# Inverse tables turned on GpSimd and transposed behind the filter's transposing DMAs, with another order of staging buffers

## The chip, the cores and the metric

The kernel runs on one core of a Trainium2 chip. The metric is device time in microseconds (us) of one launch. Three runs of the kernel before took 195.03, 194.29 and 194.93 us, so the median is 194.93 us.

The core's engines are named as in the profile: PE is TensorE (matmuls; PEld are its weight loads), DVE is VectorE, ACT is ScalarE, POOL is GpSimd, SP is SyncE, which here only issues DMAs. Each engine works through its own list in order, and waits for the others by semaphores.

## The reference, cut to what matters

With x = q of 2048 rows and 512 columns, in bf16:

```
xn = layernorm(q)
kv = causal_conv4(k, shift_k) * v                    # 4 taps along the sequence, per column
y  = irfft(rfft(kv, 4096) * rfft(ssm_k, 4096))[:2048]  # a long convolution per column
s  = xn * (y + kv * ssm_D)
h  = gelu_tanh(xn @ w_gate) * (xn @ w_up)            # 512 -> 1792
out = q + s * silu(h @ w_down)                       # 1792 -> 512
```

## The kernel before, in words

**Two halves on one PE.** The gated feed-forward part takes the 2048 rows in four quarters `q` of 512 rows and the 1792 columns in 14 tiles `m`. `unit(q, m)` (L1109) makes the gate and the up product in one PSUM bank each; ACT turns the gate bank into `GE` by gelu (L1137), and DVE multiplies the up bank by `GE` into `HT` (L1140), which frees the up bank and the `GE` slot. `down(q)` (L1143) multiplies `HT` by `Wd`. The long convolution is a two-stage Fourier transform made of matmuls. Stage 1 multiplies by `F1`: `stage1_h` (L929) for the filter, in units `H0` to `H7` and `J0` to `J7` (the two halves of the filter's columns), and `stage1_k` (L956) for `kv`. Each unit is copied from PSUM into a staging buffer and sent to HBM (`ZH`, `ZK`); stage 2 reads it back in another order and multiplies by 32x32 tiles of the table `TF` (`fwd`, L1031). The inverse multiplies by the table `MI` (L1094).

**The tables.** DVE makes `TF` (L717). `m_turn` (L726) makes from it `TFA` and `TFB`, four operations of 128x512 elements each, of which the second negates. A transposing DMA on SP turns `TFA` into `MI[:, 0]` and another one turns `TFB` into `MI[:, 1]` (L1036 to L1040); a third makes `G1` from `F1`. All three signal one semaphore, `d_g1`, and `Trk.dma` (L213) lets a DMA wait until the one before it on its semaphore has landed.

**The filter.** Filter rows come as `Hn` (four tiles, in the bytes of `G`). Two of the four are transposed by PE (`HTr`). The other two are copied by ACT into `HP` (L894) and transposed by two DMAs on SP into `HTD` (L899), one for each half `hf`; the `J` units read `HTD`.

**The taps.** SP loads the four taps to all partitions as `SKR`; POOL copies one tap at a time into `SKB[:, j]`, j = 3, 2, 1, 0 (L986). `kshift(i)` (L988) multiplies and adds on DVE for four row tiles: `KAC = KK * SKB3` (L1005), then for j = 2, 1, 0 `KTM = KK * SKBj` (L1009) and `KAC += KTM` (L1011). `KTM` has the same bytes as `SKR`:

```
skr_at = kac_at + 8192          # SKR, 4096 bytes a partition
KAC = new("KAC", [128, 2, 4, DM], BF16)   # 8192 bytes from kac_at
KTM = new("KTM", [128, 1, 4, DM], BF16)   # the 4096 bytes behind them
```

So `Trk._need` (L137) lets the first write of `KTM` wait for the last read of `SKR`, which is the copy of tap 0.

**The order of the work.** Every step is a numbered task. The string `SEQ` (L27) lists all of them in the order in which they are emitted; each engine's list is that order, cut to the engine's tasks. A planner (`Sched.run`, L345) goes through `SEQ` with estimated times, and picks buffer slots and PSUM banks by them: the slot that came free earliest. Loads are issued by SP too (`load`, L594). The tasks that matter here:

- 146, 147, 148, 149 (POOL): the copies of taps 3, 2, 1, 0; 150 (DVE): `KAC` of `kshift(0)`; 151: its first `KTM`; 152: the add behind it
- 402, 404 (PE, DVE): the up product of unit (0, 6) and its product into `HT`; 410 (PE): the up product of unit (0, 8), which the plan puts into the bank that 404 frees; 415 (ACT): the gelu of unit (0, 9), which takes the `GE` slot that 404 frees
- 81 (ACT): `m_turn`
- 61, 62 (SP): the DMAs into `HTD`; 183, 184 (SP): the transposing DMAs from `TFA` and `TFB` into `MI`; 182: the one into `G1`
- 44, 43, 41, 40, 42, 45 (SP): the loads of V2, KK3, Wd0, V1, Wd1, KK4 behind 62; 166 (DVE): `KAC` of `kshift(2)`, which needs KK3

**Staging buffers.** The `H` units use four buffers in tiles 8 to 15 of `X`. The `J` units have four as well, in the order of the list `ast["J"]` (L485): two in `X` (tiles 12 and 14) and two in `G` (tiles 4 and 6, the bytes of an `Hn` tile that PE has read by then). `J` units are evicted in the order 4, 6, 7, 2, 1, 3, 5, 0.

Of the kernel before, what the change touches and what calls it, by code (L numbers as in the profile page):

```python
# [10 lines left out]
ACTF = mybir.ActivationFunctionType  # L11
# [14 lines left out]
ORDER = "x02 h0 h1 x22 w0 w1 h2 h3 D0 w2 s0 k0 v0 x1 w3 k1 v1 d0 d1 k2 v2 k3 v3 x2 x3"  # L26
SEQ = (  # L27
# [22 lines left out]
)  # L50
NF_BANKS = 4
ISSUE = 470.0
# [29 lines left out]
class Trk:  # L82
# [29 lines left out]
    def res(self, name, ap):  # L112
        t = ap.tensor
        tn = type(t).__name__
        if tn.startswith("SB"):
            key = "SB"
            addr = self.nc.lookup_mloc(t).addr
        else:
            assert tn.startswith("PS")
            key = "PS:" + t.name  # L120
            addr = 0
        esz = mybir.dt.size(ap.dtype)
        pairs = [list(q) for q in ap.ap]
        pst, pn = pairs[0]
        pstart = ap.offset // pst if pst else 0
        inner = ap.offset - pstart * pst
        hi = sum(st * (n - 1) for st, n in pairs[1:])
        r = Res(name, key, pstart, pstart + pn, addr + inner * esz, addr + (inner + hi + 1) * esz)
        lst = self.res_by_key.setdefault(key, [])
        for o in lst:  # L130
            if o.plo < r.phi and r.plo < o.phi and o.blo < r.bhi and r.blo < o.bhi:
                o.ovl.append(r)
                r.ovl.append(o)
        lst.append(r)
        return r
# [263 lines left out]
def build_kernel(nc, A_q, A_k, A_v, A_shift_k, A_ssm_k, A_ssm_D, B_w_gate, B_w_up, B_w_down, out):  # L399
    with ExitStack() as es0:  # L400
# [11 lines left out]
        def new(name, shape, dt):  # L412
            h = at(name, shape, dt, place["at"])
            place["at"] += size(shape, dt)
            return h
# [4 lines left out]
        X = new("X", [128, NT, DM], BF16)  # L420
# [24 lines left out]
        G = new("G", [128, NT, DM], BF16)  # L445
# [36 lines left out]
        def quarter(T, j):  # L482
            return T[:, j:j + 2, :].rearrange("p x (y d) -> p (x y) d", d=256).rearrange("p (r c) d -> p r c d", c=2)

        ast = {"H": [quarter(X, j) for j in (8, 10, 12, 14)], "J": [quarter(T, j) for T, j in ((X, 12), (X, 14), (G, 4), (G, 6))],  # L485
               "K": [AST[:, j, :, :, :] for j in range(2)] + [ASX[:]]}

        ZH = nc.dram_tensor("ZH", [NG, 128, DM], BF16, kind="Internal")
# [15 lines left out]
        trk = Trk(nc, block)  # L504
        S = Sched()
# [18 lines left out]
        R_F1, R_G1, R_MF, R_MFA, R_MFB = res("F1", F1[:]), res("G1", G1[:]), res("TF", TF[:]), res("TFA", TFA[:]), res("TFB", TFB[:])  # L524
# [82 lines left out]
        def copy(e, h, o, i, scale=1.0):  # L607
            if e == "ACT":
                return h.activation(o, i, ACTF.Copy, scale=scale)  # L609
            if scale != 1.0:  # L610
                return h.tensor_scalar(o, i, scale, None, ALU.mult)
            return h.tensor_copy(o, i)  # L612
# [15 lines left out]
        bF1, bG1, bMF, bMI, bid, bSKB = B("F1"), B("G1"), B("TF"), [B(f"MI{i}") for i in range(2)], B("id"), [B(f"SKB{j}") for j in range(4)]  # L628
# [97 lines left out]
        def m_turn(e):  # L726
            tf, ta, tb = (T[:].rearrange("p g (b c) -> p (g b) c", c=2) for T in (TF, TFA, TFB))
            for o, i, f, R in ((ta[:, :, 0], 0, 1.0, R_MFA), (ta[:, :, 1], 0, -1.0, R_MFA), (tb[:, :, 0], 1, 1.0, R_MFB), (tb[:, :, 1], 1, 1.0, R_MFB)):
                trk.op("ACT", lambda h, o=o, i=i, f=f: h.activation(o, tf[:, :, i], ACTF.Copy, scale=f), r=[R_MF], w=[R])

        bFP, bQ, bMQ, bMF2 = B("fp"), B("q"), B("mq"), B("mf2")
        bFM = B("fm")
# [159 lines left out]
        for hf in range(2):  # L892
            for k in range(2):
                h_perm.append(op([("ACT", act(1024, True)), ("DVE", dve(1024, 1))], lambda e, h, hf=hf, k=k: copy(e, h, HP[:, 8 * hf:8 * hf + 8, k, :], Hn[:, 2 + k, :].rearrange("p (a t) -> p t a", t=NT)[:, 8 * hf:8 * hf + 8, :]),  # L894
                                 r=[bHn[2 + k]], w=[bHP[hf]], rr=[R_Hn[2 + k]], ww=[R_HP[hf]]))
        for hf in range(2):
# [8 lines left out]
           r=[bHD, *[bHTr[k][0] for k in range(2)]], w=[bFold], rr=[R_D, *R_HTr[0]], ww=R_HTr[0])  # L905
        op([("DVE", 420.0)], lambda e, h: h.tensor_tensor(HD0, HD0, Drow[:, 256:512], ALU.add),
           r=[bHD, bHTD[0]], w=[bFoldD], rr=[R_D, R_HTD[0]], ww=[R_HTD[0]])
        ln(0)
        S.add([("ACT", 2400.0)], m_turn, r=[bMF], w=[bMF2])
        for t in tm_tasks:  # L910
            S.behind(t, [d for b in bXN[0:4] for d in b.writers])
        xn_transpose(0)
# [310 lines left out]
        for j in range(6):  # L1223
# [7 lines left out]
                  r=[b2], w=[B(f"out{j}")], nbytes=262144)  # L1231
# [12 lines left out]
def bass_recurrent_scan__ssm_conv_h3__glu_gated_geglu__prompt_kernel(  # L1244
    nc: bass.Bass,
    A_q: bass.AP,
    A_k: bass.AP,
    A_v: bass.AP,
    A_shift_k: bass.AP,
    A_ssm_k: bass.AP,  # L1250
    A_ssm_D: bass.AP,
    B_x: bass.AP,
    B_w_gate: bass.AP,
    B_w_up: bass.AP,
    B_w_down: bass.AP,
    out: bass.AP,
):
    build_kernel(nc, A_q, A_k, A_v, A_shift_k, A_ssm_k, A_ssm_D, B_w_gate, B_w_up, B_w_down, out)
# [28 lines left out]
```

## Time and profile before

| what | value |
|---|---|
| median of three runs | 194.93 us (194.29 to 195.03) |
| span of the profiled execution | 193.3 us, so about 1.6 us of a run lie around the span |
| busy: PE, DVE, ACT, POOL | 188.6, 160.0, 125.4, 13.9 us |
| granted TensorE clock | 1.000 |
| HBM read, written | 27.39 MB, 14.68 MB |

The page gives one profiled execution. A row of a timeline has the start in us from the span's start, the length in us, the engine, the line of the kernel, the operation, what it writes and reads, and how many instructions were merged; in brackets stands the idle time of the engine just before it and what ended that. Rows named SPq or ACTq are issues of DMAs. In a row of a tile, three numbers are the shortest, the median and the longest in ns.

### The profile page before, as it was taken

How to read it: one execution, taken by the hardware profiler on the slowest of the kernel's cores; microseconds unless marked ns; L12 is line 12 of the kernel's file. 1: busy time of each engine (PE TensorE's matmuls, PEld its weight loads, DVE VectorE, ACT ScalarE, POOL GpSimd, SP SyncE). 2: the span in 40 equal slices, each digit the busy share in tenths (PEclk: the TensorE clock that was granted, in tenths of full speed). 3: DMA queues.
4: the chain of work that ended last, by engine and by line, in shares of the span. 5: the costliest groups of instructions: out<-in, count | busy, mean ns of one | idle time of the engine just before them, and what ended most of it. 6: DMA issues, size and time to landing. Idle time of an engine off the chain costs nothing.

```text
span 193.3 us, 3502 instructions
## 1 busy us (share of the span) xinstructions
PE 188.6 (98%) x1377; PEld 85.6 (44%) x1377; DVE 160.0 (83%) x245; ACT 125.4 (65%) x170; POOL 13.9 (7%) x32
## 2 busy tenths in 40 slices
PE   7899999999999999999999999999999999999993
PEld 2685544444444444443434433433444334444452
DVE  6699789998999995877888789878897863588993
ACT  6787999969885987868548766856577431232121
POOL 5412420000000000020300000000000000000000
PEclk9999999999999999999999999999999999999999
DMA  5999999999999679999999991984805345939333
GB/s 175 311 307 349 377 400 347 157 249 372 375 374 354 196 264 259 390 323 305 218 285 230 338 320 59 288 276 147 264 10 195 106 140 153 389 112 353 132 139 136
DMA packets 45958, 49.19 MB, mean 254 GB/s; under 512 B 12787, under 2 KB 39671, under 8 KB 45942
## 3 DMA queue, kind: packets, MB, share of 16 engines
q1 hardware_dynamic: 37366, 42.67, 70.1%
q10 hardware_dynamic: 8576, 6.29, 10.3%
q8 instruction: 11, 0.18, 0.4%
q14 instruction: 5, 0.04, 0.1%
HBM read 27.39 MB, written 14.68 MB: 218 GB/s over the span
## 4 chain that ended last, share of the span: by engine, by line
PE 93%; DMA 4%; SPq 1%; DVE 1%; ACT 0%; issue 0%
PE psall L618 86%; PE psall L1028 5%; DMA Hn<-in_A_ssm_k_dram 4%; PE psall L854 1%; SPq L590 1%; PE psall L878 1%; DVE G L1175 0%; DVE G L1174 0%; ACT G L1172 0%
## 5 line engine op out<-in xcount | busy, mean ns | idle before, releaser
L618 PE MATMUL psall<-xnT,Wu 128*128 128x512 bf16 (+1 forms) x232 | 55.8, 372 | 0.0
L618 PE MATMUL psall<-xnT,Wg 128*128 128x512 bf16 (+1 forms) x232 | 55.3, 372 | 0.0
L618 PE MATMUL psall<-Wd,HT 128*128 128x512 bf16 (+2 forms) x238 | 52.0, 367 | 0.0
L1140 DVE TENSOR_TENSOR HT<-psall,GE 128x512 bf16<-128x512 f32 x54 | 36.7, 685 | 15.8 <-PE psall L618 15.4
L1137 ACT ACTIVATE GE<-psall 128x512 bf16<-128x512 f32 x54 | 31.7, 601 | 13.1 <-PE psall L618 12.9
L618 PEld LDWEIGHTS psall<-Wd,HT 128*128 128x128 bf16 x238 | 22.4, 98 | 25.9 <-issue 1.1
L618 PEld LDWEIGHTS psall<-xnT,Wg 128*128 128x128 bf16 x232 | 21.9, 98 | 25.4 <-issue 1.3
L618 PEld LDWEIGHTS psall<-xnT,Wu 128*128 128x128 bf16 x232 | 21.6, 98 | 25.9 <-issue 3.5
L609 ACT ACTIVATE X<-psall 128x1024 bf16<-128x1024 f32 (+1 forms) x18 | 15.1, 843 | 3.3 <-DMA ZH<-X 1.9
L609 ACT ACTIVATE HS<-psall 128x1024 bf16<-128x1024 f32 x14 | 13.7, 1022 | 4.4 <-PE psall L1028 4.4
L1164 ACT ACTIVATE G<-psall 128x512 bf16<-128x512 f32 x12 | 7.0, 598 | 12.9 <-PE psall L618 12.4
L1011 DVE TENSOR_TENSOR KAC<-KAC,KTM 128x2048 bf16<-128x2048 bf16 x12 | 14.6, 1217 | 0.1
L1009 DVE TENSOR_TENSOR KTM<-KK,SKB 128x2048 bf16<-128x2048 bf16 x12 | 14.6, 1217 | 0.0
L609 ACT ACTIVATE BO<-psall 128x1024 bf16<-128x1024 f32 x9 | 9.1, 1022 | 8.2 <-PE psall L1028 7.7
L609 ACT ACTIVATE KB<-psall 128x1024 bf16<-128x1024 f32 x11 | 11.0, 1021 | 3.6 <-PE psall L1028 3.6
L609 ACT ACTIVATE AST<-psall 128x1024 bf16<-128x1024 f32 x12 | 12.4, 1033 | 0.7 <-PE psall L618 0.5
L612 DVE CAST BO<-psall 128x1024 bf16<-128x1024 f32 x7 | 8.5, 1224 | 3.7 <-PE psall L1028 3.7
L821 DVE BATCH_NORM_STATS2 stats<-X 128x6 f32<-128x512 bf16 x16 | 10.3, 675 | 1.1 <-DMA X<-in_A_q_dram 1.1
L1172 ACT ACTIVATE G<-psall 128x512 bf16<-128x512 f32 (+2 forms) x5 | 2.6, 512 | 13.1 <-PE psall L618 13.1
L1091 DVE TENSOR_TENSOR HW<-KB,HW 128x1024 bf16<-128x1024 bf16 x16 | 10.9, 682 | 0.0
L1091 DVE TENSOR_TENSOR HS<-KB,HS 128x1024 bf16<-128x1024 bf16 x16 | 10.8, 682 | 0.0
L1166 DVE SCALAR_TENSOR_TENSOR G<-G,psall 128x512 bf16<-128x512 bf16 x12 | 7.8, 680 | 2.0 <-ACT G L1164 2.0
(83 smaller groups left out, 175.6 us busy)
## 6 DMA issues: line engine op xcount, KB each, us to landing
BH<-ZH SPq DMA_DIRECT2D x8, 512.0 KB, 6.1
HW<-HS SPq DMA_DIRECT2D x16, 256.0 KB, 3.2
BK<-ZK SPq DMA_DIRECT2D x8, 512.0 KB, 5.1
ZI<-BO ACTq DMA_DIRECT2D x16, 256.0 KB, 2.8
BI<-ZI SPq DMA_DIRECT2D x8, 512.0 KB, 4.2
ZK<-AST SPq DMA_DIRECT2D x6, 512.0 KB, 4.1
Hn<-in_A_ssm_k_dram SPq DMA_DIRECT2D x4, 512.0 KB, 8.4
KK<-in_A_k_dram SPq DMA_DIRECT2D x4, 512.0 KB, 8.6
```

What stands on the lines that cost most here:

```text
L609: return h.activation(o, i, ACTF.Copy, scale=scale)
L612: return h.tensor_copy(o, i)
L618: return h.matmul(o, lhsT=l, rhs=r, start=st, stop=sp)
L821: t_stats[t] = op([("DVE", 670.0)], lambda e, h, t=t: h.bn_stats(stats[:, t, :], X[:, t, :]), r=[bX[q][t % 4]], w=[bst[t]], rr=[R_X[t]], w ...
L1009: op([("DVE", dur)], lambda e, h, j=j, m=m: h.tensor_tensor(KTM[:, m.slot, :, :], kk(j), sk(j), ALU.mult), r=need + [bSKB[j], a], w=[m], r ...
L1011: op([("DVE", dur)], lambda e, h, m=m: h.tensor_tensor(KAC[:, a.slot, :, :], KAC[:, a.slot, :, :], KTM[:, m.slot, :, :], ALU.add), r=[m], ...
L1028: trk.op("PE", lambda h: h.matmul(ps(s, i)[b, :], lhsT=wt(col)[a, :], rhs=data(col)[a, :], start=n < 16, stop=n >= len(todo) - 16, tile_po ...
L1091: return hd.tensor_tensor(o, flat(KB, kb[h]), o, ALU.mult)
L1137: op([("ACT", act(512))], lambda e, h: h.activation(GE[:, g.slot, :], bank(pg), ACTF.Gelu_apprx_tanh), r=[pg], w=[g], rr=lambda: R_bank(pg ...
L1140: op([("DVE", dve(512, 1))], lambda e, h: h.tensor_tensor(HT[:, q % 2, m, :], bank(pu), GE[:, g.slot, :], ALU.mult), r=[pu, g], w=[bHT[q][m]],
L1164: op([("ACT", act(n))], lambda e, h, g=g, pc=pc: h.activation(g, pc(), ACTF.Tanh, scale=0.5), r=[p], w=[bt], rr=lambda p=p: R_bank(p), ww= ...
L1166: op([("DVE", dve(512, 1))], lambda e, h, g=g, pc=pc: h.scalar_tensor_tensor(out=g, in0=g, scalar=1.0, in1=pc(), op0=ALU.add, op1=ALU.mult ...
```

## The change

Three edits. `m_turn` is emitted to POOL instead of ACT, by the helper `copy` (L607), which makes a copy for the factor 1.0 and a `tensor_scalar` with a multiplication for -1.0. In `SEQ`, task 81 goes from behind 430 to between 147 and 148; 183 goes to right behind 61, and 184 to right behind 62. All else in `SEQ` keeps its order (the string is only broken into lines at other places). The `J` units' list of buffers begins with the two in `G`.

```
 SEQ = (
...
-    ... 430 81 477 ...      ... 140 183 45 508 ...      ... 137 184 241 ...
+    ... 396 99 147 81 121 466 148 468 150 ... 149 151 ...
+    ... 417 61 183 423 424 106 429 156 97 114 158 93 60 62 184 431 44 ...
...
-        ast = {"H": [quarter(X, j) for j in (8, 10, 12, 14)], "J": [quarter(T, j) for T, j in ((X, 12), (X, 14), (G, 4), (G, 6))],
+        ast = {"H": [quarter(X, j) for j in (8, 10, 12, 14)], "J": [quarter(T, j) for T, j in ((G, 4), (G, 6), (X, 12), (X, 14))],
...
         def m_turn(e):
             tf, ta, tb = (T[:].rearrange("p g (b c) -> p (g b) c", c=2) for T in (TF, TFA, TFB))
             for o, i, f, R in ((ta[:, :, 0], 0, 1.0, R_MFA), (ta[:, :, 1], 0, -1.0, R_MFA), (tb[:, :, 0], 1, 1.0, R_MFB), (tb[:, :, 1], 1, 1.0, R_MFB)):
-                trk.op("ACT", lambda h, o=o, i=i, f=f: h.activation(o, tf[:, :, i], ACTF.Copy, scale=f), r=[R_MF], w=[R])
+                trk.op("POOL", lambda h, o=o, i=i, f=f: copy("POOL", h, o, tf[:, :, i], f), r=[R_MF], w=[R])
...
-        S.add([("ACT", 2400.0)], m_turn, r=[bMF], w=[bMF2])
+        S.add([("POOL", 2600.0)], m_turn, r=[bMF], w=[bMF2])
```

43 rows, old and new, of the table SEQ are left out of this document.

## The prediction

> **What bounds the kernel now.** I read the page first, its busy times and its chain, and then the table of busy times in stretches of 10 us.
>
> ```profile
> PE 188.6 (98%) x1377; PEld 85.6 (44%) x1377; DVE 160.0 (83%) x245; ACT 125.4 (65%) x170; POOL 13.9 (7%) x32
> ...
> PE 93%; DMA 4%; SPq 1%; DVE 1%; ACT 0%; issue 0%
> ```
>
> ```profile
> 20.00:30.00 10.00, 10.00 (x60) 5.03 (x59) 8.07 (x12) 9.37 (x15) 3.41 (x4) 1.00 1.07 392
> 30.00:40.00 10.00, 10.00 (x52) 4.68 (x50) 10.00 (x12) 10.00 (x13) 0.00 (x0) 1.00 0.98 237
> 40.00:50.00 10.00, 10.00 (x48) 4.54 (x47) 9.17 (x11) 8.26 (x13) 0.00 (x0) 1.00 1.06 331
> 50.00:60.00 10.00, 10.00 (x48) 4.57 (x47) 10.00 (x11) 7.65 (x11) 0.00 (x0) 1.00 1.11 361
> ```
>
> In the second fence the columns after the length are PE, PEld, DVE, ACT and POOL, then the granted clock and the DMA share. PE is the chain, and it is busy in all of each stretch in which the change does anything, at a granted clock of 1.00. The change leaves PE's list as it is. So time that is freed on ACT, or in the DMA queue, has no hole on PE to fill; but each moment for which the change holds PE back is lost for good, because nothing later has slack to give it back. The question is therefore not what ACT saves, but whether anything that PE waits for comes later than it may.
>
> **Part 1: the four operations move from ACT to POOL, between the copies of taps 2 and 1.** What ACT gives up:
>
> ```profile
> L729 ACT ACTIVATE TFA<-TF x2: 774/778/783, 42.7 to 43.5; 128x512 bf16<-128x512 bf16 x2
> ```
>
> Four operations of about 0.78 are 3.1 us of ACT from 42.7 on. PE is full there, so this is worth nothing.
>
> What POOL has, and what DVE does next to it:
>
> ```profile
> 17.09 0.24 POOL L831 TENSOR_SCALAR mv<-mv 128x4 f32<-128x4 f32 x1 [6.45 <-DVE mv L822]
> 17.42 1.05 POOL L832 TENSOR_TENSOR mv<-mv,NHALF 128x4 f32<-128x4 f32 x1
> 21.85 3.41 POOL L986 COPY SKB<-SKR 128x512 bf16<-128x512 bf16 x4 [3.39 <-DMA SKR<-in_A_shift_k_dram]
> ```
>
> ```profile
> L986 POOL COPY SKB<-SKR x4: 637/646/1658, 21.9 to 23.6; 128x512 bf16<-128x512 bf16 x4
> ```
>
> ```profile
> 23.32 1.42 DVE L1005 TENSOR_TENSOR KAC<-KK,SKB 128x2048 bf16<-128x2048 bf16 x1
> 24.66 0.68 DVE L1140 TENSOR_TENSOR HT<-psall,GE 128x512 bf16<-128x512 f32 x1
> 25.30 1.22 DVE L1009 TENSOR_TENSOR KTM<-KK,SKB 128x2048 bf16<-128x2048 bf16 x1
> 27.45 0.69 DVE L1140 TENSOR_TENSOR HT<-psall,GE 128x512 bf16<-128x512 f32 x1 [0.94 <-PE psall L618]
> 28.06 1.22 DVE L1011 TENSOR_TENSOR KAC<-KAC,KTM 128x2048 bf16<-128x2048 bf16 x1
> 29.19 0.68 DVE L1140 TENSOR_TENSOR HT<-psall,GE 128x512 bf16<-128x512 f32 x1
> ```
>
> The copies start 0.58 apart and take 0.64. The last one starts at 23.60 and takes 1.66: it ends at 25.26, as if it had begun only at 24.62, when the `KAC` multiplication that started at 23.32 was about done. So POOL's copy stands still while DVE multiplies two SBUF operands.
>
> The Trainium skill has a rule for that ("SBUF — State Buffer", section "Who interferes with whom"): a DVE instruction with two SBUF inputs and a GpSimd instruction that reads SBUF shut each other out for a whole instruction. The two rows agree with it; by it alone the moved operations could also hold DVE's multiplications back.
>
> Now the wait that matters. The `KTM` row at 25.30 is task 151, and it starts 0.04 after the last copy's end at 25.26. That is no accident: `KTM` has the bytes of `SKR`, so its first write waits for the copy of tap 0, the last on POOL's list, although it needs only tap 2. Behind it on DVE stands 404 (27.45), the product that frees the bank of the up product 410. In the kernel before, DVE has 0.94 to spare ahead of 404. The change puts four more operations ahead of the copy of tap 0.
>
> POOL's list worked out anew, with X for the second operation, the `tensor_scalar`:
> - Taps 3 and 2 as before. Operation 1 takes the place of tap 1: 23.02 to 23.66.
> - Operation 2 writes the same tile and waits for operation 1. A POOL operation that waits for the one before starts 0.09 after its end (17.09 + 0.24, then 17.42), so at 23.75; the `KAC` multiplication then holds it to 24.62, as it held tap 0. It ends at 24.62 + X.
> - Operation 3 ends 0.58 later (25.20 + X), operation 4 waits for it and ends at 25.93 + X.
> - Tap 1 ends at 26.51 + X, tap 0 at 27.09 + X. `KTM` starts at 27.13 + X instead of 25.30.
>
> DVE has nothing else that it may do: 404 stands behind `KTM`. DVE's next operation starts 1.13 after such a multiplication (28.06, then 29.19), and 404 takes 0.69, so 404 ends at 28.95 + X.
>
> ```profile
> 29.02 1.03 PE L618 MATMUL psall<-xnT,Wu 128*128 128x512 bf16 x4
> ```
>
> ```profile
> 74.40 1.02 ACT L609 ACTIVATE ASX<-psall 128x1024 bf16<-128x1024 f32 x1 [0.81 <-PE psall L618]
> ```
>
> ```profile
> 75.47 0.28 PEld L618 LDWEIGHTS psall<-V,F 128*128 128x128 bf16 x2 [0.15 <-ACT ASX L609]
> ```
>
> The PE row is 410. How soon PE follows: where a load waited for ACT's end at 75.42, it started at 75.47; with some 0.2 from a load to its matmul, I estimate 0.25 from the freeing to the matmul. PE would start 410 at 29.20 + X, and it started at 29.02. **The stall is 0.18 + X.**
>
> X is not in the trace: no POOL `tensor_scalar` with 512 elements.
>
> ```profile
> L663 POOL TENSOR_SCALAR ident<-K 128x128 bf16<-128x128 int32 x1 | 0.6, 568 | 0.0
> ...
> L831 POOL TENSOR_SCALAR mv<-mv 128x1 f32<-128x1 f32 x4 | 0.9, 224 | 3.4 <-DVE mv L822 3.4
> ```
>
> From 1 to 128 elements the `tensor_scalar` grows by 344 ns, 2.7 ns an element; 512 elements would take 1.6 us. From below, the copy of as many elements takes 0.64. It can't take less than a copy, which leaves no gain here. The first is a comparison of int32 and the second is no arithmetic; a bf16 multiplication lies between them, and I take the middle, X = 1.1. The stall is 0.82 with the low end, 1.28 with mine, 1.8 with the high one. The three copies of `m_turn` step over every second element on both sides, the tap copies over four on one side; I take the tap's 0.64 for them, and if each took 0.2 more, 0.6 would be added, which is the upper part of my range.
>
> The Trainium skill's "GPSIMD Engine Reference", section "Engine selection", calls one-input operations on GpSimd roughly line-rate; by that X would be at the low end, and the time 195.75. No run here shows it for a `tensor_scalar`.
>
> What is late behind it: 415 waits for the `GE` slot that 404 frees, so ACT falls back by about as much, and DVE too. Their products then lie against a PE that is late by the same amount, so I count the stall once. DVE's later multiplications meet POOL no more, as POOL is done.
>
> **Part 2: the transposing DMAs.** They are behind the filter's on SP, ahead of six loads.
>
> ```profile
> 32.08 6.18 SPq L899 DMA_TRANSPOSE HTD<-HP  x2
> 38.30 1.51 SPq L590 DMA_DIRECT2D V<-in_A_v_dram  x1
> 39.87 0.48 SPq L590 DMA_DIRECT2D KK<-in_A_k_dram  x1
> ...
> 44.33 5.69 SPq L1039 DMA_TRANSPOSE MI<-TFA  x1
> ...
> 54.57 2.61 SPq L1039 DMA_TRANSPOSE MI<-TFB  x1
> ...
> 61.81 1.32 SPq L1039 DMA_TRANSPOSE G<-F  x1
> ```
>
> ```profile
> KK<-in_A_k_dram SPq DMA_DIRECT2D x1, 512.0 KB, 6.3
> ```
>
> ```profile
> HTD<-HP SPq DMA_TRANSPOSE x2, 5.3
> ```
>
> ```profile
> 36.00:37.00 1.00, 1.00 (x6) 0.42 (x5) 1.00 (x2) 1.00 (x3) 0.00 (x0) 1.00 0.26 54
> ```
>
> ```profile
> 48.67 1.22 DVE L1005 TENSOR_TENSOR KAC<-KK,SKB 128x2048 bf16<-128x2048 bf16 x1
> 49.81 1.22 DVE L1011 TENSOR_TENSOR KAC<-KAC,KTM 128x2048 bf16<-128x2048 bf16 x1
> 50.94 0.68 DVE L1140 TENSOR_TENSOR HT<-psall,GE 128x512 bf16<-128x512 f32 x1
> ```
>
> ```profile
> 52.77 1.03 PE L618 MATMUL psall<-xnT,Wg 128*128 128x512 bf16 x4
> ```
>
> An issue into `MI` took 2.61 and 5.69 in a loaded queue, the four times smaller one into `G1` 1.32; the queue is lighter here (a DMA share of 0.26 at 36), so I take 1.3 to 2.6. The two issues move the loads back by 2.6 to 5.2. The second one also waits for the first one's landing on their one semaphore, and the loads stand behind that wait: with 5.3 to landing, as for `HTD`, it lies mostly under the issues of the first (1.3 or more) and of the second `HTD` DMA (half of 6.18), and about 1 is left over. So the loads are issued up to 6.2 later.
>
> KK3 has the nearest need: 39.87 + 6.3 is 46.2, and DVE multiplies by it at 48.67, which leaves 2.5. DVE's next product ends at 51.62, its bank is taken at 52.77, and with my 0.25 that leaves 0.9 more until PE feels it. With the forecast's stall, DVE comes 1.3 later by itself. So KK3 may be 4.7 late. Its 6.3 to landing were spent behind the `HTD` transpose and V2; the transposes into `MI` now partly use the idle queue of 36. I expect it to land 2 to 4 later and take zero; the upper bound is 6.2 - 4.7 = 1.5. The other loads are needed later than KK3, and KK4 no longer has the `MI` issue of 5.69 in front of it.
>
> **Part 3: buffers.**
>
> ```profile
> 57.87 1.02 ACT L609 ACTIVATE X<-psall 128x1024 bf16<-128x1024 f32 x1 [0.96 <-DMA ZH<-X]
> ```
>
> ACT waits such as this one, for a staging buffer's store to land, become shorter: J4 and J6, evicted first, take `G` tiles, and their stores find a shorter queue. The reverse, J7 and J2 waiting for an `X` tile, comes later, when more stores have landed. PE is full at 57.87 all the same, and such a wait is under 1 us of an engine that PE doesn't wait for there: zero both ways.
>
> **Sum.** The span of 193.3 becomes 193.3 + 1.3 = 194.6; with the 1.6 us around it that is **196.2 us**, against the median of 194.93 (slower by 0.7%).
>
> **The rivals.** A difference under 0.5% (1.0 us, the runs lie within 0.74) can't be told from none.
>
> *X at its low end.* The stall is 0.82 and the time 195.75, which counts as no change. For it: the copy's row. Against: the 568 ns for 128 elements. 0.18.
>
> *The wait doesn't reach PE*, because the plan's altered times give 410 another bank, or another up product is enough ahead: 194.9. Against it: the bank of 404 is the longest free one in the plan by a step, and an altered POOL time of 0.2 in the plan is small. 0.08.
>
> *KK3 late.* PE's stall comes as in the forecast, and at 50 DVE waits again, for KK3. It decides when the load is issued more than 4.7 later and still takes 6.3; from nothing to 1.5 is added, in the middle 0.8: 197.0. For it: two issues and a landing ahead of it. Against: a queue with less in it. 0.10.
>
> *Faster.* Where the rows of waits say that PE's loads wait for ACT,
>
> ```profile
> PEld psall L1028 <- ACT GE L1137: 4.7, 11, 0.4
> ...
> PEld psall L1028 <- issue: 3.8, 9, 0.4
> ```
>
> an ACT with 3.1 us less to do could take away half of the 4.7: 192.6. It decides if these are true waits. But the gap is 0.4 whichever cause is named, even with none; so I read it as the cost of going from 128-row to 32-row tiles. 0.04.
>
> **How the numbers follow.** The forecast has 0.60 (a stall from 0.9 to 2.4: 195.8 to 197.3). Slower by over 0.5%: the forecast nearly whole, and KK3: 0.69. Within 0.5%: the low X, no reach, and the forecast's edge: 0.27. Faster: 0.04. The range from 195.3 to 197.3 holds the forecast, the low X and part of KK3's.
>
> **What would show it.** In the profile after: POOL's run from 21.85 ends near 28.2 instead of 25.26; `KTM` at about 28.2, and the wait list has DVE `KTM` on POOL with some 2.9; a hole on PE at 29.0 of about 1.3, and the chain passes there from PE through DVE to POOL. The `KK` row at 39.87 comes at 43 to 46, and DVE does not wait for it. I am wrong if PE has no hole at 29, or if X is below 0.64; and right by luck if a hole of this size lies elsewhere.

## The result, and the profile after

Five runs of the changed kernel took 196.86 to 198.56 us, median 197.45; five of the kernel before, beside them, 194.29 to 195.03, median 194.73. The ratio is 1.0141 (95% interval 1.0104 to 1.0177): the change makes the kernel slower by 2.7 us. The profiled execution is the shortest of the five, 196.86 us with a span of 195.0. All lines of the changed kernel stand one number higher than before.

The page of the changed kernel, its busy times and its chain:

```profile
PE 187.5 (96%) x1377; PEld 84.7 (43%) x1377; DVE 159.8 (82%) x245; ACT 122.6 (63%) x166; POOL 17.5 (9%) x36
...
PE 77%; DMA 11%; SPq 4%; POOL 4%; ACT 2%; issue 1%; DVE 1%; ACTq 0%
```

PE had 93% of the chain before and has 77% now: the chain leaves PE, for POOL and for DMAs. The waits of PE and DVE say at which rows (total us, times, longest):

```profile
PE psall L619 <- DVE HT L1141: 1.7, 1, 1.7
...
PE psall L619 <- ACT G L610: 0.3, 1, 0.3
...
DVE KTM L1010 <- POOL SKB L987: 3.6, 1, 3.6
```

None of the three was there before. The chain, in order of time (start, length, what):

```profile
21.26 1.23 POOL SKB L987 x2
22.48 0.71 POOL TFA L613
...
23.27 2.45 POOL TFA L612
25.73 0.69 POOL TFB L613
...
26.46 0.76 POOL TFB L613
27.23 1.15 POOL SKB L987 x2
...
28.39 0.04 DVE KTM L1010
28.43 1.11 issue
29.54 0.70 DVE HT L1141
30.23 0.05 issue
30.28 1.04 PE psall L619 x4
...
50.52 0.92 ACT G L610
...
51.46 8.79 DMA ZH<-G
...
60.33 1.03 ACT G L610
...
61.41 2.76 PE psall L619 x12
```

It leaves PE twice after 28 us. The first time it is the forecast's path: POOL's list up to the copy of tap 0, `KTM`, the product 404, and PE's up product 410 at 30.28. The second time it is a path that I had set to zero: ACT evicts J4 into a `G` tile (50.52), the store of that tile lands at 60.25, only then ACT evicts J1 into the same tile (60.33), and PE gets the bank at 61.41. PE's timeline at the two places:

```profile
28.16 0.39 PE L855 MATMUL psall<-ident,XN 128*128 128x128 bf16 x4
30.28 1.04 PE L619 MATMUL psall<-xnT,Wu 128*128 128x512 bf16 x4 [1.73 <-DVE HT L1141]
...
60.08 1.03 PE L619 MATMUL psall<-xnT,Wg 128*128 128x512 bf16 x4
61.41 0.61 PE L619 MATMUL psall<-V,F 128*128 128x512 bf16 x2 [0.30 <-ACT G L610]
```

A group of four long matmuls shows 1.03, but where nothing waits the next one starts 0.86 after it, since the ends are modelled. So a hole, the time in which PE does nothing, is the idle time in the brackets and 0.17 more: 1.90 and 0.47, together 2.37. This execution was earlier than the one before by 0.64 when it came to 410 (due at 30.28 - 1.90 = 28.38, against 29.02), and 2.37 - 0.64 is the 1.7 by which the spans differ.

SP's timeline shows what stands ahead of that store in the queue, first two rows of the kernel before (KK4 and J4's store, there out of an `X` tile), then those of the changed kernel:

```profile
50.06 0.58 SPq L590 DMA_DIRECT2D KK<-in_A_k_dram  x1
...
51.21 0.47 SPq L590 DMA_DIRECT2D ZH<-X  x1
```

```profile
35.51 1.75 SPq L1040 DMA_TRANSPOSE MI<-TFA  x1
...
41.07 1.37 SPq L1040 DMA_TRANSPOSE MI<-TFB  x1
42.48 1.67 SPq L591 DMA_DIRECT2D V<-in_A_v_dram  x1
44.21 0.44 SPq L591 DMA_DIRECT2D KK<-in_A_k_dram  x1
...
46.39 3.55 SPq L591 DMA_DIRECT2D KK<-in_A_k_dram  x1
...
51.46 0.38 SPq L591 DMA_DIRECT2D ZH<-G  x1
```

The load of V2, the first behind the transposes, is issued at 42.48 instead of 38.30. KK4 (46.39) is issued 3.7 earlier than before (50.06), and yet lands later: it takes 11.9 us to landing where it took 5.8, so at 58.3 against 55.9. J4's store lands 2.0 behind it. From 40 to 60 the DMA share is 1.04 to 1.16 in each stretch of 5 us before, and 1.07 to 1.20 after: I take it that the queue is full there, and that what goes ahead in it delays all that stands behind. The runs below show which DMA delays the store, and not how.

### The profile page after: what moved, and what is told of

Read it like the earlier page. It is cut to its first block, busy times and chain, and to the rows that moved or that the text cites. A ratio compares the mean times of both kernels' runs of the same rounds, so it can differ in the third digit from the quotient of the medians.

```text
span 195.0 us, 3503 instructions
## 1 busy us (share of the span) xinstructions
PE 187.5 (96%) x1377; PEld 84.7 (43%) x1377; DVE 159.8 (82%) x245; ACT 122.6 (63%) x166; POOL 17.5 (9%) x36
## 4 chain that ended last, share of the span: by engine, by line
PE 77%; DMA 11%; SPq 4%; POOL 4%; ACT 2%; issue 1%; DVE 1%; ACTq 0%
PE psall L619 71%; DMA SKR<-in_A_shift_k_dram 6%; PE psall L1029 5%; DMA ZH<-G 5%; SPq L591 4%; POOL TFA L612 1%; POOL SKB L987 1%; ACT G L610 1%; POOL TFB L613 1%; POOL TFA L613 0%; DVE HT L1141 0%; ACT GE L1138 0%; DVE G L1176 0%; DVE G L1175 0%; ACT G L1173 0%
## 5 line engine op out<-in xcount | busy, mean ns | idle before, releaser
L1138 ACT ACTIVATE GE<-psall 128x512 bf16<-128x512 f32 x54 | 31.7, 601 | 18.3 <-PE psall L619 13.8
L619 PEld LDWEIGHTS psall<-Wd,HT 128*128 128x128 bf16 x238 | 22.4, 98 | 25.9 <-issue 1.1
L610 ACT ACTIVATE X<-psall 128x512 bf16<-128x512 f32 (+1 forms) x14 | 11.0, 793 | 0.3 <-PE psall L619 0.3
```

Source lines behind the costliest of these rows:

```text
L619: return h.matmul(o, lhsT=l, rhs=r, start=st, stop=sp)
L1138: op([("ACT", act(512))], lambda e, h: h.activation(GE[:, g.slot, :], bank(pg), ACTF.Gelu_apprx_tanh), r=[pg], w=[g], rr=lambda: R_bank(pg ...
```

## The experiments

Theory 1: the first `KTM` has the bytes of `SKR` and waits for the whole of POOL's list. Theory 2: the transposes ahead of the loads make KK3 and, above all, J4's store land late. Rival A: POOL's work beside DVE's multiplications is the price in itself. Rival B: the order of the J buffers makes ACT wait. Ratios are against the kernel before, which was run beside them (medians 194.41 to 194.59).

**Taps first: task 81 behind the copies of taps 1 and 0**

```
-    ... 99 147 81 121 466 148 468 150 ... 149 151 ...
+    ... 99 147 121 466 148 468 150 ... 149 81 151 ...
```

> The four operations of m_turn stay on POOL, but behind the copies of taps 1 and 0. Theory 1 (the first KTM waits for the copy of tap 0, because it writes the bytes of SKR): tap 0's copy ends at about 25.3 again, KTM starts right behind it, the hole of 1.89 us on PE at 28.3 is gone, and the time falls by about 1.9 to 195.5 us. Rival A (POOL's work beside DVE's multiplications is the price in itself, wherever it lies on the list): the operations now lie beside more of those multiplications, a hole of about the same size comes a little later, and the time stays near 197.4. Theory 2 has the second hole of about 0.5 at 60.7 stay as it is.

Measured: 196.36 us, ratio 1.0092 (1.0062 to 1.0121). The first hole is gone (410 starts at 28.39, behind PE's work without a gap). But only about 1 of the 1.9 us came back. The timeline shows where the rest went, PE's rows first, then one of DVE and one of ACT:

```profile
50.85 1.03 PE L618 MATMUL psall<-xnT,Wu 128*128 128x512 bf16 x4
51.71 0.59 PE L618 MATMUL psall<-HTD,F 128*128 128x512 bf16 x2
52.50 1.04 PE L618 MATMUL psall<-xnT,Wg 128*128 128x512 bf16 x4 [0.20 <-DVE HT L1140]
...
54.24 1.04 PE L618 MATMUL psall<-xnT,Wg 128*128 128x512 bf16 x4 [0.26 <-DVE HT L1140]
...
49.48 1.23 DVE L1005 TENSOR_TENSOR KAC<-KK,SKB 128x2048 bf16<-128x2048 bf16 x1 [1.35 <-DMA KK<-in_A_k_dram]
...
59.96 1.02 ACT L609 ACTIVATE G<-psall 128x1024 bf16<-128x1024 f32 x1 [2.44 <-DMA ZH<-G]
```

Now DVE waits 1.35 for KK3, which opens two small holes on PE (0.37 and 0.43), and the hole behind J1's eviction has grown from 0.47 to 1.2: 2.0 in all, where the median is 1.9 above. With the first hole in place PE and DVE came later, and the late load and most of the late store had been hidden behind it.

**`SKR` apart**

```
-        skr_at = kac_at + 8192
+        skr_at = kac_at - 12 * 1024
```

> Only the place of SKR changes: 8 KB of its own, which nothing writes until much later, so KTM no longer waits for the copy of tap 0 and needs only tap 2's. POOL's list and every operation on it stay. Theory 1: POOL is as long as before and ends near 28.4, KTM starts at about 24 to 25.5 (behind KAC and 404), the first hole on PE is gone; the second multiplication by KK needs tap 1 at 27.8 and the third tap 0 at 28.4, which may cost some tenths: 195.5 to 196.0 us. Rival A: POOL holds DVE back as in the changed kernel, the hole stays, 197.4.

Measured: 196.45, ratio 1.0083 (1.0055 to 1.0111). DVE's row of the first `KTM`:

```profile
25.00 1.21 DVE L1010 TENSOR_TENSOR KTM<-KK,SKB 128x2048 bf16<-128x2048 bf16 x1
```

It starts while POOL still works on the table, and no hole at 28 is left, with POOL's list as long as in the change. So the false dependence makes that hole, not POOL's work. The time again stays 2 us above: holes of 0.7 and 0.4 behind KK3 and of 1.0 behind the store, 2.1 in all.

**The transposing DMAs back**

```
-    ... 61 183 423 ... 62 184 431 ... 140 45 ... 137 241 ...
+    ... 61 423 ... 62 431 ... 140 183 45 ... 137 184 241 ...
```

> Only the two transposing DMAs into MI go back to their old places in SP's list; the four operations stay where the change put them on POOL. Theory 1: the first hole on PE stays at 1.9 us. Theory 2 (these DMAs push the loads back, and the store of J4 behind the loads): the loads are issued from about 38 on again, the store of the first G quarter lands about 1.2 us earlier, and the second hole of 0.46 is gone: 197.0 us. Rival B (the order of the J buffers is what makes ACT wait for a landing): the second hole stays, 197.4.

Measured: 196.42, ratio 1.0094 (1.0064 to 1.0124). A row of PE's waits, then ACT's eviction of J1, and PE's rows at the bank that it frees:

```profile
PE psall L618 <- DVE HT L1140: 2.1, 1, 2.1
```

```profile
59.84 1.02 ACT L609 ACTIVATE G<-psall 128x1024 bf16<-128x1024 f32 x1 [1.24 <-PE psall L618]
```

```profile
60.49 1.03 PE L618 MATMUL psall<-xnT,Wg 128*128 128x512 bf16 x4
61.36 0.59 PE L618 MATMUL psall<-V,F 128*128 128x512 bf16 x2
```

The first hole is whole (2.3) and the second one is gone. ACT's row names PE, but it is still the store that ACT waits for: it lands at 59.75, and ACT starts 0.09 later, as in the changed kernel (60.25, then 60.33). The eviction ends at 60.86, and PE, late by the first hole, takes the bank only at 61.36, without a gap. So the store is late here too, and no longer costs anything. I had expected it 1.2 earlier than in the changed kernel (it is 0.5) and the time at 197.0; taking the second hole away gave back about 1 us.

**No negation: the second operation a copy (the sign of `TFA`'s odd elements is left out)**

```
-            for o, i, f, R in (... (ta[:, :, 1], 0, -1.0, R_MFA), ...):
+            for o, i, f, R in (... (ta[:, :, 1], 0, 1.0, R_MFA), ...):
```

> The second operation of m_turn becomes a plain copy like the other three; the sign of the odd elements of TFA is left out of the computation. Theory 1 with the size of X as the miss: the operation takes about 0.75 instead of the 1.64 that remain after the wait for DVE's multiplication, tap 0's copy ends 0.9 earlier, the first hole shrinks from 1.9 to 1.0 and the time to 196.5. Rival A' (the 2.45 us are a lock by DVE and not the operation's own work): the copy in its place ends at about the same time, the hole stays at 1.9, 197.4.

Measured: 196.91, ratio 1.0112 (1.0084 to 1.0141). POOL's row of the first two operations:

```profile
22.80 2.42 POOL L613 COPY TFA<-TF 128x512 bf16<-128x512 bf16 x2
```

The first one takes 0.77, the second starts at 23.63 and ends at 25.22: 1.59 where the `tensor_scalar` took 2.45, behind the same `KAC` multiplication. A strided copy alone takes 0.76 (the second into `TFB`, in the chain above). If the `tensor_scalar` stood still beside that multiplication as the copy did, its own work is 0.76 + 2.45 - 1.59 = 1.62 us; it could also take 2.45 and have stood still for nothing. The first hole shrinks from 1.9 to 0.9, but one of 0.4 opens behind KK3, and the one behind J1's eviction grows from 0.5 to 1.1: 2.4 in all, as in the changed kernel.

**The same with the transposes back**

> Transposing DMAs at their old places, and the second operation a plain copy (the sign of TFA's odd elements is left out), so that the first hole is the only one and its size can be read in the time. Theory: the operation's own work falls from about 1.64 to 0.76, and the time by 0.9 against the kernel with the DMAs alone put back, to about 1.0 to 1.1 us above the kernel before. If the second hole were still hidden behind the first, less than 0.5 would be gained.

Measured: 196.07, ratio 1.0069 (1.0043 to 1.0095). PE's wait at 410 is 1.3 instead of 2.1, so 0.8 smaller, where I had expected 0.9. The time isn't as expected: the median is only 0.35 lower than with the negation, and 1.5 above the kernel before instead of 1.0 to 1.1. The intervals are as wide as that difference, so the time alone settles nothing here, and the trace is what bears X.

**The changed kernel again**

> The changed kernel as it is, on the chip of the next three, to compare them with. Both theories: 2.3 to 2.7 us above the kernel before.

Measured: 197.74, ratio 1.0153 (1.0124 to 1.0181), so 3.0 us above by the ratio, a little more than expected. Its profiled execution has the same two paths with longer waits, 2.1 for DVE's `HT` and 0.8 for ACT's `G`, and the store lands at 61.67.

**Both repairs, in two ways**

Taps first, or `SKR` apart, each with the DMAs back; engine, operations and J order stay as changed.

> Both repairs at once: the four operations stay on POOL but behind the copies of taps 1 and 0, and the two transposing DMAs are back at their old places on SP. What is left of the change is the engine and the order of the J buffers. The theory that there are two walls, one behind the other (the copy of tap 0 at 28, the loads and the store behind the transposes at 50 to 60, each worth about 2 us alone, 2.4 to 2.7 together): both gone, within 0.4 us of the kernel before. Rival A (POOL beside DVE costs in itself) or rival B (the order of the J buffers): about 1 to 2 us above the kernel before remain.

> The other pair of repairs: SKR has 8 KB of its own, the operations stand on POOL where the change put them, and the two transposing DMAs are back at their old places. Theory of two walls: within 0.5 us of the kernel before, although POOL's list is as long and as early as in the changed kernel. Rival A or B: 1 to 2 us above the kernel before remain.

Measured: 194.46, ratio 1.0002 (0.9981 to 1.0023), and 194.49, ratio 1.0000 (0.9980 to 1.0020). PE's chain with `SKR` apart is one piece from 29.33 on, through both places:

```profile
29.33 36.70 PE psall L618 x171
```

Rival A has fallen: the four operations stand on POOL as early as in the change and cost nothing. So the two paths are the whole loss, to within some 0.4 us, and ACT's freed 3.1 us are no gain that these runs could show.

**The table first: task 81 ahead of all four taps, the DMAs back.** In all runs above the `tensor_scalar` began beside a DVE multiplication of two SBUF operands. Here it does not, and that tells the two readings apart.

```
-    ... 146 394 405 396 99 147 81 121 ...
+    ... 81 146 394 405 396 99 147 121 ...
```

> The four operations stand ahead of all four taps on POOL, from about 18.8 on (the table is ready at 18.75, SKR lands near 21.2), where DVE runs no multiplication of two SBUF operands; the transposing DMAs are at their old places. If the tensor_scalar takes 1.62 by its own work and stood still beside DVE's multiplication as a copy does, it now takes 1.6 and the four end at about 22.4; if it takes 2.45 by itself and never stood still, it takes 2.45 here too and they end at 23.2. Tap 0's copy then ends at 24.9 to 25.7 or so, against 25.26 in the kernel before, and 410 has no hole or one of a few tenths: within 0.5 us of the kernel before either way.

Measured: 194.50, ratio 1.0007 (0.9989 to 1.0025). POOL's timeline:

```profile
20.12 1.68 POOL L611 TENSOR_SCALAR TFA<-TF 128x512 bf16<-128x512 bf16 x1
21.71 1.74 POOL L612 COPY TFB<-TF 128x512 bf16<-128x512 bf16 x2
23.36 3.42 POOL L986 COPY SKB<-SKR 128x512 bf16<-128x512 bf16 x4
```

It takes 1.68 without such a neighbour: 1.6 to 1.7 is its own work, and the rest of the 2.45 was standing still. Tap 0's copy ends at 26.78, 1.1 later than the latest that I had expected: the four operations end at 23.45 instead of 22.4, and a tap's copy stands still beside `KAC`, as in the kernel before. PE has no hole at 410 all the same.

**The J buffers**

```
-  ... for T, j in ((G, 4), (G, 6), (X, 12), (X, 14))],     # with SKR apart
+  ... for T, j in ((X, 12), (X, 14), (G, 4), (G, 6))],
```

> SKR apart, the transposing DMAs early as in the change, and the J buffers in their old order (X tiles first). Theory of two walls: ACT's wait of about 2.3 us for a landing store stays, now on an X tile, and so do the holes on PE near 52 and 60: as with SKR apart alone, some 2 us above the kernel before. Rival B (G tiles first make ACT wait): the hole of 1.0 at 60 goes and the time falls by about 1 us against SKR apart alone.

> The kernel before with only the order of the J buffers changed (G tiles first). Theory of two walls: no effect, within 0.3 us of the kernel before. Rival B: up to 1 us slower.

Measured: 196.35, ratio 1.0086 (1.0064 to 1.0109), with the old order beside early transposes; 194.50, ratio 0.9994 (0.9976 to 1.0011), with the new order alone. With the old order ACT waits for a store out of `X` instead, and the hole at 60 is 1.05, as with the new one. Rival B has fallen: the order of the buffers makes no difference that these runs show.

**One transpose early, or both behind five loads (`SKR` apart)**

```
one back:     ... 61 183 423 ... 62 431 ... 137 184 241 ...
pair behind:  ... 61 423 ... 62 431 ... 140 183 184 45 ...
```

> SKR apart; the first transposing DMA into MI stays early, only the second goes back to its old place. Then the loads stand behind one issue and no landing: about 2.3 us later than at the old places, not 4.5; and the last load of KK and the store of J4 no longer stand behind an issue of 7 us. Theory of two walls, in which the loads' and the store's lateness is what costs: the load of KK3 lands before 48, the store before 58, both holes gone, within 0.4 us of the kernel before. If already one of them ahead of the loads costs, 0.5 to 1.5 us remain.

> SKR apart; both transposing DMAs behind the first five of the six loads, the second right behind the first, so ahead of the last load of KK and of the store of J4. If KK3's lateness made the holes near 52, these go; if the store's landing makes the hole near 60, it grows: the second transpose waits for the first one's landing (53.7 at these places), so KK4 and the store are issued some 5 us later and the store lands at about 62 to 64 instead of 57: 3 to 6 us above the kernel before. If only the late loads cost: within 0.5 us of it.

Measured, one back: 195.05, ratio 1.0012 (0.9992 to 1.0032), no hole: the first transpose may be early. The store lands 2.3 earlier than with `SKR` apart alone (57.5 against 59.9), and only the place of the second transpose tells the two kernels apart. Pair behind: 201.49, ratio 1.0349 (1.0317 to 1.0381), 6.8 above, which is more than expected (the last section has the rest). KK3 is in time there and PE has no hole near 52, but SP's and PE's rows show this:

```profile
42.76 7.90 SPq L1039 DMA_TRANSPOSE MI<-TFA  x1
54.79 1.23 SPq L1039 DMA_TRANSPOSE MI<-TFB  x1
56.06 0.58 SPq L590 DMA_DIRECT2D KK<-in_A_k_dram  x1
...
57.17 0.43 SPq L590 DMA_DIRECT2D ZH<-G  x1
...
64.27 0.94 PE L618 MATMUL psall<-V,F 128*128 128x512 bf16 x2 [4.68 <-ACT G L609]
```

The second transpose waits until the first has landed (54.77), KK4 and J4's store wait behind it, the store lands at 63.11, and PE stands for 4.85. So the store is enough by itself.

**One rule for the second path.** In a table, with 410's due time (its start less the hole just ahead of it), the landings of KK4 and of J4's store, the store's distance from 410's due time, and the holes on PE from 28 to 62:

| kernel | 410 due | KK4 lands | store lands | store behind 410 | holes |
|---|---|---|---|---|---|
| before | 29.02 | 55.9 | 57.8 | 28.8 | none |
| both repairs (`SKR` apart) | 28.08 | 55.1 | 57.0 | 28.9 | none |
| one back | 28.24 | 55.6 | 57.5 | 29.3 | none |
| both repairs (taps first) | 27.92 | 55.7 | 57.6 | 29.7 | 0.2 |
| taps first | 28.39 | 57.9 | 59.9 | 31.5 | 2.0 |
| `SKR` apart | 28.12 | 57.9 | 59.9 | 31.7 | 2.1 |
| DMAs back | 28.43 | 57.9 | 59.75 | 31.3 | 2.3, all at 28 |
| changed | 28.38 | 58.3 | 60.25 | 31.9 | 2.4 |
| no negation | 28.91 | 58.9 | 60.9 | 31.9 | 2.4 |
| changed, again | 28.93 | 59.7 | 61.7 | 32.7 | 3.2 |
| pair behind | 28.77 | 61.0 | 63.1 | 34.3 | 4.85 |

The store lands 1.9 to 2.1 behind KK4 in every kernel, and where it is the store that holds PE up, the holes up to 62 are its distance less 29.5 or 29.6, wherever they lie. So in the changed kernel the store sets the sum (31.9 - 29.5 = 2.4), and the first hole of 1.9 is part of it and not on top. In the row of the DMAs put back the store would make holes of 1.8, and the first hole alone is larger; there the first hole sets the sum.

## Why the prediction was right and where it was wrong

**What bounds, and ACT's time: right.** PE is the bound, and 3.1 us less on ACT gave nothing: with both repairs the time is that of the kernel before, to within some 0.4 us.

**The wait: right.** POOL's list ends at 28.36, `KTM` starts 0.03 later, and PE's hole lies ahead of 410. That this is a matter of bytes and not of POOL's work is shown by `SKR` apart.

**The size of the stall: too small, 1.28 against 1.90.** The term is X: I took the middle, 1.1, between a copy's 0.64 and the 1.6 worked out from 128 elements; it is 1.62 to 1.68, at the upper end or just above it (+0.5). The strided copies took 0.76 and not 0.64, which makes the last four operations 0.17 longer. Against that PE follows 0.05 after 404's end and not 0.25 (-0.2). The rest, 0.1, is in the starts. The Trainium skill ("GPSIMD Engine Reference", "Engine selection") has one-input operations on GpSimd at roughly line rate. The trace doesn't agree for the `tensor_scalar`, which has one input and took more than twice the copy's 0.76.

**The loads: right for KK3.** KK3 lands at 49.9, 3.7 later, where I wrote 2 to 4 later; with the stall in place DVE takes it at 49.94 with nothing lost, as the rival's condition said. The two issues into `MI` took 1.75 and 1.37, as I had taken, and the first one had landed (39.19) before the second was issued. Without the stall KK3 costs 0.8 (taps first) to 1.1 (`SKR` apart).

**The buffers: this step failed.** In Part 3 I called ACT's wait for a landing store "zero both ways", as shorter than 1 us and of an engine that PE doesn't wait for there, and in Part 2 I dismissed KK4 because no transpose is issued just ahead of it. The first holds only while the store lands in time: PE takes over the bank that J1's eviction frees, and the store may land some 29.5 behind 410's start, 0.7 later than it did before. In the changed kernel it landed 3.1 later (31.9 against 28.8). The second took the time of issue for the time of landing. I followed the loads to their readers on DVE, and not to the store that stands in the same queue behind them. The first hole, and the late loads with the store, each make a loss of 1.8 to 2 by themselves (DMAs back, and taps first), and together the store sets the sum: with a copy in the place of X the time is still 2.2 us above (1.0112), where my low-X rival had 0.8. It took both terms to leave the range that I gave: with either one mended the time lies within it (196.91 and 196.42).

**Rivals.** The wait does reach PE. Nothing became faster: the row of PEld's waits for ACT that this rival rested on stands at 4.7 in the changed kernel too. KK3's rival was there, but hidden.

**Open.** The two series of the changed kernel are 2.7 and 3.0 above the kernel before; the first profile, of the shortest run, shows 2.4 of holes; the second, of the longest run of its series, shows 3.2. Why the store lands at 60.25 in one profiled execution and at 61.67 in another was not tried, and neither was how the second transpose, ahead in the queue, makes KK4 and the store land late.

## What to carry to other kernels

Where an engine is full, two late events do not add up: each sets an earliest time, and the later one counts. So taking one away gives back less than its hole (here 1.0 of 1.9), and what a repair is worth shows only with the other one repaired as well. When a DMA is moved ahead in a queue, follow every DMA behind it to its landing and to whoever waits for that, stores and the buffers they release among them; an earlier issue can land later, as KK4's did. And look for tiles that share bytes: a reader that nobody thinks of as urgent can hold back the writer of the next tile.

## What the runs showed of the hardware that I had not expected

**A `tensor_scalar` on POOL costs more than twice a copy:** 1.68 us against 0.76 for 128x512 bf16, every second element on both sides.

**DVE and POOL hold each other back both ways, but not always.** With both repairs (`SKR` apart), the timeline of DVE and then that of POOL:

```profile
22.31 1.50 DVE L1005 TENSOR_TENSOR KAC<-KK,SKB 128x2048 bf16<-128x2048 bf16 x1
...
24.34 1.21 DVE L1009 TENSOR_TENSOR KTM<-KK,SKB 128x2048 bf16<-128x2048 bf16 x1
...
22.02 0.77 POOL L612 COPY TFA<-TF 128x512 bf16<-128x512 bf16 x1
22.88 2.46 POOL L611 TENSOR_SCALAR TFA<-TF 128x512 bf16<-128x512 bf16 x1
```

The `KAC` multiplication starts in the middle of a POOL copy and takes 0.29 longer than `KTM`, where the copy had 0.48 to go; the `tensor_scalar` starts in the middle of `KAC` and stands still until it is done. The Trainium skill ("SBUF — State Buffer", "Who interferes with whom") says that whoever comes first shuts the other out; these rows agree in kind. But `KTM` starts in the middle of the `tensor_scalar` and is not held back at all, which the rule does not have. It is the same with `SKR` apart, one back and pair behind, 1.21 each time, while the `KTM` that starts in the middle of a copy (taps first) takes 1.70. POOL's spans are rough, and no run was made to find the reason.

**A long hole costs more than its length.** In the kernel with the pair behind, the table of busy times (PE, PEld, DVE, ACT, POOL, granted clock, DMA share, GB/s):

```profile
60.00:64.30 4.30, 0.03 (x1) 0.04 (x2) 3.24 (x4) 1.02 (x1) 0.00 (x0) 1.00 1.01 350
64.30:68.00 3.70, 3.70 (x10) 1.39 (x11) 3.67 (x4) 1.65 (x2) 0.00 (x0) 0.54 0.58 204
68.00:74.00 6.00, 6.00 (x30) 2.70 (x29) 3.76 (x5) 4.72 (x7) 0.00 (x0) 1.00 0.68 195
```

After the hole of 4.85 the granted clock is 0.54 for 3.7 us, which adds about 1.7 to it: 6.5 of the 6.8 us by which this kernel is slower. The holes of up to 2.3 in the other profiles left the clock at 1.00. The Trainium skill ("TensorE: Matmul & The Clock Gate", "Why this matters for your kernels") warns of idle gaps of over some 3 us; the runs agree, with none between 2.3 and 4.85.
